# One group of value read-outs a pair, four buffers of each kind of exponentials, one dump tile, stack loads in odd steps

## The chip, the cores and the metric

The kernel runs on one core of a Trainium2 chip. The metric is the device time in microseconds (us) of one execution; each median below is over several executions. Beside the times there is one execution taken by the hardware profiler. The engines are TensorE (PE in the profile, with PEld for its weight loads), VectorE (DVE), ScalarE (ACT), GpSimd (POOL) and SyncE (SP). SP does no arithmetic here: it issues nearly all DMAs. SBUF is the on-chip memory of 128 partitions, PSUM the small memory that TensorE writes, in 8 banks of 128x512 fp32.

## What is computed

One transformer block on x of 2048 rows by 512 columns: modulated layer norm, attention with 32 heads of 16 columns in four segments of 512 rows, and a feed-forward part of width 1792. The part that matters here is the attention inside a segment:

```python
for s in range(N):                                   # 4 segments of L = 512 rows
    qs, ks, vs = q[:, :, s], k[:, :, s], v[:, :, s]
    logits = jnp.einsum("bhqd,bhkd->bhqk", qs, ks) * scale + mask
    p = _softmax(logits, axis=-1)
    a_dot = jnp.einsum("bhqk,bhkd->bhqd", p, vs)
    ...
    o = g * a_mem + (1.0 - g) * a_dot
```

## The kernel before

**Three parts.** Part A (up to about 190 us) makes q, k and v of all segments and writes q and k, split into three bf16 terms, to DRAM (`QD`, `KD`). Part B (about 180 to 480 us) is the attention above, with the output projection of finished segments and the preparation of the feed-forward part woven in. Part C is the feed-forward part. The change lies in part B alone.

**Steps and pairs.** Part B runs 64 steps P, four before them and two after; a step is two heads of one segment. Q = P // 2 numbers *pairs* of steps: four heads that share one stack of q rows and one of k rows (`qst`, `kst`, 96 rows of 2048 bf16, five buffers each, `NK = 5`). Eight pairs make a segment. What is issued in a step follows a list written out by hand, `PRM['order']` (lines 25 to 34): two lists for each segment, one for even and one for odd steps. Its tokens are

- `S0` to `S3` (`s_part`, line 623): the logits of step P + 4, with queries on the partitions, and their maximum over the keys. For each of the blocks 3, 2 and 1 of queries and each of the two heads TensorE makes a product of 512, 384 or 256 columns (line 610) and VectorE takes its masked maximum (`masked_max`, line 615): six maxima a step. Block 0 of all four heads shares a bank, a mask product and one plain maximum (`s_mask`, line 651), once a pair.
- `T0` to `T4` (`st_part`, line 702): the logits of step P again, keys on the partitions, with the maximum subtracted through three further rows of `qst` (lines 696 and 715); ScalarE writes their exponential into SBUF tiles `pts` of three kinds, GpSimd zeroes the causal triangle (line 699). Kind `pt0` holds key block 0, `pt1` blocks 1 and 3, `pt2` block 2.
- `c0` to `c9`: places for all else. Each item has a position, `ap(pos, f)`: step pos // 10, place pos % 10.

All `S` and `T` products rotate through six PSUM banks `att`. A bank is used again once its reader (VectorE for S, ScalarE for T) is done.

**The maximum and its dump tile.** `masked_max` is one VectorE operation that adds the mask, takes the minimum of the negated values into an accumulator and writes the elementwise result, which nobody reads, to a bf16 tile `dump`. On the engine it is two records: the operation itself (`CUSTOM_DVE_ANT_0`) and the read of the accumulator into `nm` (`DVE_READ_ACCUMULATOR2_ANT`), which raises VectorE's semaphore. The two tiles `dump0` and `dump1` take turns. In the instruction stream of the kernel before, a maximum waits for the count that the accumulator read of the maximum *two before it* raises, that is, for the last writer of its own dump tile; where it waits for TensorE too, that wait stands in an EVENT_SEMAPHORE instruction of its own ahead of it.

**The value read-out** (`pv_part`, line 731): for pair Q and key block j, four products, one for each head, of the exponentials with a 128x32 slice of `V`, each in its own 32 columns of the array and so beside one another; each fp32 product is two matmul instructions. Key block 0 has 512 columns, blocks 1, 2 and 3 have 384, 256 and 128. All accumulate in the bank `pvb`. `pv` lists for each segment the position (relative to 20 Q), key block and columns of the four blocks. With the table of before they form three separate runs on TensorE in the first segment (blocks 0 and 3; 2; 1) and two in the others (0 and 3, then 2 and 1; 0 and 2, then 1 and 3; 0, then 2, 1 and 3); the last pair forms one. `pv_out` (745, position `pvout`) copies the bank to `ts` on ScalarE and stores it to DRAM (`TD`); `pv_in` (753) loads two pairs back turned, `den` (773) makes the inverse denominator and stores it (`RD`), `rb_in` (782) loads it spread out.

**The row of maxima** (`m_rows`, 667, and `m_put`, 673): the maxima of pair Q, turned by TensorE, are copied by ScalarE to `ms` (48x128) and sent by a small DMA on ScalarE's own queue into rows 96 to 98 of `qst`, in step 2Q - 2. The first `T` of step 2Q needs it.

**The stack loads** (`load_stacks`, 190): `kst` and `qst` of pair Q, 384 KB each, from DRAM on SP, at position 20 Q + `stacks`. The first `S` that reads them stands in step 2Q - 4; the buffers' last readers are the `T` of step 2Q - 9. SP works its queue off in order and runs ahead of the steps as far as the waits allow.

Of the kernel before, what the change touches and what calls it, by code (L numbers as in the profile page):

```python
# [8 lines left out]
F32 = mybir.dt.float32  # L9
F32R = mybir.dt.float32r  # L10
BF16 = mybir.dt.bfloat16
# [23 lines left out]
 'turn': 2,  # L35
# [4 lines left out]
 'pvout': [41, 35, 34, 33],  # L40
 'mrows': [-21, -21, -25, -22],
 'mput': [-14, -15, -13, -13],
 'mrow0': -19,
 'mput0': -9,
 'stacks': -80,
 'den': [84, 84, 84, 84],
 'dnl': 11,
 'rbl': 7,
# [54 lines left out]
NEG = -1e30  # L103
# [3 lines left out]
def block_kernel(ctx: ExitStack, tc: tile.TileContext, x, wq, wk, wv, wo, betaq, betam,  # L107
                 w1, b1c, w2, b2, ccol, wmod, maskbd, mask8, out):
    nc = tc.nc
    v, act, pool, pe, sp = nc.vector, nc.scalar, nc.gpsimd, nc.tensor, nc.sync  # L110
# [7 lines left out]
    maskb = per.tile([128, 512], BF16, name="maskb")  # L118
# [101 lines left out]
    with ExitStack() as pa:  # L220
# [124 lines left out]
        for ds in ((0,), (1, 2, 3)):  # L345
# [4 lines left out]
            n = slice(ds[0], ds[-1] + 1)  # L350
# [180 lines left out]
        for s in range(NSEG):  # L531
            for tok in PRM["A"][s].split():
                n = int(tok[1]) if len(tok) > 1 and tok[1].isdigit() else 0
# [54 lines left out]
    with ExitStack() as pb:  # L588
        sb = pb.enter_context(tc.tile_pool(name="sb", bufs=2, reuse_waits="tile"))
# [15 lines left out]
        def bank():  # L605
            turn[0] += 1
            return att[turn[0] % 6]
# [1 line left out]
        def s_mm(ps, P, h, i):  # L609
            pe.matmul(ps, q_of(P, h, i), k_of(P, h, 128 * (i + 1)), start=True, stop=True)  # L610

        dump = [sb.tile([128, 512], BF16, name=f"dump{i}", bufs=1) for i in range(2)]
        n_dump = [0]

        def masked_max(dst, src, n):
            n_dump[0] += 1
            v.tensor_tensor_reduce(out=dump[n_dump[0] % 2][:, :n], in0=src, in1=maskb[:, 512 - n:], scale=-1.0, scalar=-4 * NEG,  # L617
                                   op0=ALU.add, op1=ALU.min, accum_out=dst)

        def s_max(dst, src):  # L620
# [59 lines left out]
        pts = {}  # L680
        late = []
# [12 lines left out]
        def st_mm(ps, P, h, j):  # L694
            q, k, e = qst[P // 2 % NK], kst[P // 2 % NK], 2 * (P % 2) + h
            pe.matmul(ps, k[:99, e, 128 * j:128 * j + 128], q[:99, e, 128 * j:512], start=True, stop=True)  # L696

        def causal(t, pattern):
            pool.affine_select(out=t, in_=t, pattern=pattern, compare_op=ALU.is_ge, fill=0.0,  # L699
                               base=0, channel_multiplier=-1)  # L700

        def st_part(P, part):
            ps = bank()
            if part < 4:
                u, h = part // 2, part % 2
                if (P, u) not in pts:
                    pts[P, u] = late[0].tile([128, 2, 512], F32, tag=f"pt{u}", bufs=3 + u, name=f"pt{P}_{u}")
                pt = pts[P, u]
                if u == 0:
                    st_mm(ps, P, h, 0)  # L710
                else:
                    st_mm(ps[:, :384], P, h, 1)
                    st_mm(ps[:, 384:], P, h, 3)
                    pts[P, 3] = pt[:, :, 384:]
                act.activation(pt[:, h, :], ps, AF.Exp, scale=0.25)  # L715
                if h == 1:
                    causal(pt[:, :, 0:128], [[0, 2], [1, 128]])
                    if u:
                        causal(pt[:, :, 384:], [[0, 2], [1, 128]])
            else:  # L720
                pt = late[0].tile([128, 2, 256], F32, tag="pt2", bufs=4, name=f"pt{P}_2")
                pts[P, 2] = pt
                two = ps.rearrange("k (h n) -> k h n", h=2)
                for h in range(2):
                    st_mm(two[:, h, :], P, h, 2)
                act.activation(pt, two, AF.Exp, scale=0.25)
                causal(pt[:, :, 0:128], [[0, 2], [1, 128]])
# [157 lines left out]
        for Q in range(32):  # L885
            z = Q // 8
            pv = PRM["pv"][z]
# [56 lines left out]
        for P in range(-LEAD, NP + 2):  # L944
            if P in PRM["w1at"]:
                stage_w1(2 * PRM["w1at"].index(P))
            for tok in PRM["order"][2 * min(P // 16, 3) + P % 2 if P >= 0 else 8 + P % 2].split():
                n = int(tok[1])
                if tok[0] == "S":
                    if P + LEAD < NP:  # L950
                        s_part(P + LEAD, n)
                elif tok[0] == "M":
                    s_mask()
                elif tok[0] == "T":
                    if 0 <= P < NP:
                        st_part(P, n)
                else:
                    for f, a in todo.pop((P, n), ()):
                        f(*a)
# [5 lines left out]
    with ExitStack() as pc:  # L965
# [127 lines left out]
        for n in range(AHEAD, NSEG * FB + AHEAD):  # L1093
            s, f = divmod(n, FB)
# [36 lines left out]
            if n < NSEG * FB:  # L1131
                if n > AHEAD:
                    ffn1(n)
                d = f - 9
# [58 lines left out]
```

## Time and profile before

| what | value |
|---|---|
| median of 3 runs (lowest, highest) | 809.91 us (808.03, 811.72) |
| time of the profiled execution | 815.29 us |
| its span, first to last instruction | 813.4 us |
| granted TensorE clock, mean of the span | 0.994 |
| ScalarE busy, GpSimd busy | 366.1 us (45%), 282.7 us (35%) |

The span is what the views divide into windows; the profiled execution took 1.9 us more than its span, and 5.4 us more than the median of the runs. Busy times are unions of an engine's records, so an engine that is 97% busy by them can still be the one that waits for nobody or one whose records merely touch. A window's row gives, for each engine, busy time and number of records, then the granted clock, the busy share of the DMA engines and what they moved.

### The profile page before, as it was taken

The page shows a single profiled execution, that of the slowest core. Times are in us where ns is not written, and L with a number is a line of the kernel's source. Part 1 is how long each engine was busy: PE and PEld are TensorE (multiplying, and loading weights), DVE is VectorE, ACT ScalarE, POOL GpSimd, SP SyncE. Part 2 cuts the span into 40 slices and gives each one's busy share as a digit, 9 for nine tenths or more (in the row PEclk, how much of TensorE's full clock was granted, in tenths as well). Part 3 has the DMA queues.
Part 4 walks back from the last instruction along what each step waited for, and adds up shares of the span by engine and source line. Part 5 has one row for each costly group of instructions (what it writes and reads, how often), then busy time and mean ns, then how long its engine had stood idle before and what let it go on. Part 6 is the DMA issues. An engine that isn't in the chain of part 4 may idle for free.

```text
span 813.4 us, 13418 instructions
## 1 busy us (share of the span) xinstructions
PE 790.9 (97%) x4637; PEld 549.1 (68%) x4637; DVE 505.9 (62%) x1353; ACT 366.1 (45%) x671; POOL 282.7 (35%) x496
## 2 busy tenths in 40 slices
PE   9999999999998999989999998999999999999998
PEld 4877767865443455435554556788888888888887
DVE  6685696458887887788779536884542353324223
ACT  4465645565777776667678661132112111211110
POOL 1347366541477565557878650000000000000000
PEclk9999999999999999999999999999999999999999
DMA  9597756496455577767656475733020121003001
GB/s 339 176 318 244 265 184 227 154 344 189 145 155 152 161 219 212 229 177 222 185 182 177 129 221 178 225 115 106 25 79 1 52 62 43 1 0 105 1 1 52
DMA packets 83564, 123.01 MB, mean 151 GB/s; under 512 B 14116, under 2 KB 46244, under 8 KB 82984
## 3 DMA queue, kind: packets, MB, share of 16 engines
q1 hardware_dynamic: 81000, 120.19, 47.2%
q10 hardware_dynamic: 2496, 1.97, 0.8%
q8 instruction: 36, 0.59, 0.3%
q14 instruction: 32, 0.26, 0.1%
HBM read 75.60 MB, written 46.15 MB: 150 GB/s over the span
## 4 chain that ended last, share of the span: by engine, by line
PE 47%; DVE 2%; DMA 2%; ACT 1%; issue 1%; SPq 0%; POOL 0%; DVEq 0%
PE acc L1075 18%; PE f1b L991 17%; PE pvb L740 3%; PE att L696 3%; PE mm L817 3%; PE att L610 2%; PE mm L162 1%; DMA xt<-X2D 1%; DMA w2r<-in_w 1%; DMA rm<-rdd 1%; PE mm L1075 1%; DVE dump L617 0%; DVE xb L835 0%; DVE cst L149 0%; ACT pt L715 0%
## 5 line engine op out<-in xcount | busy, mean ns | idle before, releaser
L617 DVE CUSTOM_DVE_ANT_0 dump<-att,maskb 128x512 bf16<-128x512 f32 (+2 forms) x384 | 192.2, 553 | 34.0 <-PE att L610 24.3
L715 ACT ACTIVATE pt<-att 128x512 f32<-128x512 f32 x256 | 144.2, 602 | 56.3 <-PE att L696 43.7
L994 ACT ACTIVATE gt<-f1b,b1t 128x512 f32<-128x512 f32 x56 | 38.5, 688 | 244.2 <-PE f1b L991 200.4
L699 POOL TENSOR_SCALAR_AFFINE_SELECT pt<-pt 128x256 f32<-128x256 f32 x256 | 99.7, 409 | 86.8 <-ACT pt L715 54.5
L140 DVE CAST gh<-gt 128x512 fp32r<-128x512 f32 x56 | 23.8, 426 | 161.3 <-ACT gt L994 161.3
L696 PE MATMUL att<-qst,kst 99*128 99x512 bf16 (+3 forms) x512 | 108.7, 305 | 8.8 <-DMA qst<-ms 5.4
L610 PE MATMUL att<-kst,qst 96*128 96x512 bf16 (+2 forms) x384 | 91.6, 331 | 0.7 <-DVE nm L617 0.2
L1075 PE MATMUL acc<-w2h,gh 128*128 128x512 f32 (+1 forms) x224 | 86.9, 388 | 0.0
L1075 PE MATMUL acc<-w2l,gh 128*128 128x512 f32 (+1 forms) x224 | 86.1, 384 | 0.8 <-DVE w2l L141 0.8
L696 PEld LDWEIGHTS <-kst 99*128 99x128 bf16 x512 | 44.8, 98 | 61.5 <-issue 26.8
L1075 PE MATMUL acc<-w2h,gl 128*128 128x512 f32 (+1 forms) x224 | 85.7, 383 | 0.0
L740 PE MATMUL pvb<-pt,V 128*32 128x512 f32 (+2 forms) x992 | 82.1, 442 | 0.0
L991 PE MATMUL f1b<-hodd,w1h 128*128 128x512 f32 x224 | 73.7, 390 | 0.0
L153 POOL TENSOR_SCALAR crs<-cmv 128x4 f32<-128x4 f32 x4 | 1.0, 248 | 172.6 <-DVE cmv L150 172.6
L740 PEld LDWEIGHTS pvb<-pt,V 128*32 128x32 f32 x992 | 25.0, 109 | 44.0 <-issue 39.8
L610 PEld LDWEIGHTS <-qst 96*128 96x128 bf16 x384 | 33.9, 99 | 23.9 <-issue 7.7
L1075 PEld LDWEIGHTS acc<-w2l,gh 128*128 128x128 f32 x224 | 42.1, 188 | 10.0 <-DVE w2l L141 1.6
L991 PEld LDWEIGHTS f1b<-hodd,w1h 128*128 128x128 f32 x224 | 42.1, 188 | 8.5
L1075 PEld LDWEIGHTS acc<-w2h,gl 128*128 128x128 f32 x224 | 42.1, 188 | 8.4
L1075 PEld LDWEIGHTS acc<-w2h,gh 128*128 128x128 f32 x224 | 42.1, 188 | 8.2
L991 PE MATMUL f1b<-C0hh,w1h 128*128 128x512 f32 x112 | 43.7, 390 | 0.8 <-DVE w1h L140 0.8
L991 PE MATMUL f1b<-C0hh,w1l 128*128 128x512 f32 x112 | 43.8, 391 | 0.3 <-DVE w1l L141 0.3
(213 smaller groups left out, 1546.0 us busy)
## 6 DMA issues: line engine op xcount, KB each, us to landing
kst<-KD SPq DMA_DIRECT2D x32, 384.0 KB
qst<-QD SPq DMA_DIRECT2D x32, 384.0 KB
TD<-ts SPq DMA_DIRECT2D x32, 256.0 KB
QD<-q SPq DMA_DIRECT2D x16, 384.0 KB
KD<-k SPq DMA_DIRECT2D x16, 384.0 KB
wm<-in_wmod SPq DMA_DIRECT2D x20, 256.0 KB
QD<-q SPq DMA_DIRECT2D x16, 256.0 KB
KD<-k SPq DMA_DIRECT2D x16, 256.0 KB
```

The lines of the kernel that those rows point to most:

```text
L140: v.tensor_copy(hi, src)
L162: pe.transpose(ps[:, 128 * b:128 * b + 128], xh[:, b, 128 * d:128 * d + 128], ident)
L610: pe.matmul(ps, q_of(P, h, i), k_of(P, h, 128 * (i + 1)), start=True, stop=True)
L617: v.tensor_tensor_reduce(out=dump[n_dump[0] % 2][:, :n], in0=src, in1=maskb[:, 512 - n:], scale=-1.0, scalar=-4 * NEG, op0=ALU.add, op1=AL ...
L696: pe.matmul(ps, k[:99, e, 128 * j:128 * j + 128], q[:99, e, 128 * j:512], start=True, stop=True)
L699: pool.affine_select(out=t, in_=t, pattern=pattern, compare_op=ALU.is_ge, fill=0.0, base=0, channel_multiplier=-1)
L715: act.activation(pt[:, h, :], ps, AF.Exp, scale=0.25)
L740: pe.matmul(ps[32 * c:32 * c + 32, lo:hi], V[4 * s + j][:, VW * hd:VW * hd + 32], pt[:, c % 2, lo - o:hi - o], start=start, stop=stop)
L817: pe.matmul(ps, a[:, 128 * b:128 * b + 128], w[:, g, :], start=(g == 0 and i == 0), stop=(g == 3 and i == 2))
L991: pe.matmul(ps, a[:, k, :], b[k], start=(i == 0), stop=(i == 11))
L994: act.activation(g, ps, AF.Gelu_apprx_tanh, bias=b1t[:, f:f + 1])
L1075: pe.matmul((mm if lo else acc[b])[:, lo:hi], a[:, c], w[:, lo:hi], start=(f == 0 and i == 0), stop=(last and i == 2))
```

## The change

The four key blocks of a pair are read out at one place, in the odd step 2Q + 3 (place 2 in the first segment, 3 in the others), in the order 0, 2, 1, 3, and the bank is copied out at the same place. Key block 0 is thereby read up to a step later, and `pt0` gets four buffers like the other kinds (one more, 4 KB a partition). `dump` is one tile (1 KB a partition less). The stack loads move from even to odd steps: position 20 Q - 70 in place of 20 Q - 80. `pv_in` keeps its distance of 11 places behind `pv_out`; `den` and all else keep their positions.

```diff
- 'pv': [[[29, 0, 0, 512], [29, 3, 384, 512], [32, 2, 256, 512], [41, 1, 128, 512]],
-        [[28, 0, 0, 512], [28, 3, 384, 512], [34, 2, 256, 512], [35, 1, 128, 512]],
-        [[29, 0, 0, 512], [29, 2, 256, 512], [33, 1, 128, 512], [34, 3, 384, 512]],
-        [[27, 0, 0, 512], [33, 2, 256, 512], [33, 1, 128, 512], [33, 3, 384, 512]]],
- 'pvout': [41, 35, 34, 33],
+ 'pv': [[[d, 0, 0, 512], [d, 2, 256, 512], [d, 1, 128, 512], [d, 3, 384, 512]] for d in (32, 33, 33, 33)],
+ 'pvout': [32, 33, 33, 33],
...
- 'stacks': -80,
+ 'stacks': -70,
...
-        dump = [sb.tile([128, 512], BF16, name=f"dump{i}", bufs=1) for i in range(2)]
+        dump = [sb.tile([128, 512], BF16, name="dump0", bufs=1)]
...
-            v.tensor_tensor_reduce(out=dump[n_dump[0] % 2][:, :n], in0=src, in1=maskb[:, 512 - n:], scale=-1.0, scalar=-4 * NEG,
+            v.tensor_tensor_reduce(out=dump[0][:, :n], in0=src, in1=maskb[:, 512 - n:], scale=-1.0, scalar=-4 * NEG,
...
-                    pts[P, u] = late[0].tile([128, 2, 512], F32, tag=f"pt{u}", bufs=3 + u, name=f"pt{P}_{u}")
+                    pts[P, u] = late[0].tile([128, 2, 512], F32, tag=f"pt{u}", bufs=4, name=f"pt{P}_{u}")
```

## The prediction

> **What bounds the kernel now.** I read the page first. Its row of busy times has the engines in the order PE, PEld, DVE, ACT, POOL:
>
> ```profile
> PE 790.9 (97%) x4637; PEld 549.1 (68%) x4637; DVE 505.9 (62%) x1353; ACT 366.1 (45%) x671; POOL 282.7 (35%) x496
> ```
>
> TensorE is busy 97% of the span, VectorE 62%. By these averages TensorE time is what counts and VectorE is free. But part B, where the change lies, has its own balance, so I cut it into stages by the work woven in: light pairs with attention alone, and heavy ones that also carry the output projection.
>
> ```profile
> core 0 of [0], span 813.4 us
> core 0: us, PE busy (x) PEld busy (x) DVE busy (x) ACT busy (x) POOL busy (x), PEclk, DMA share, GB/s
> 208.00:295.36 87.36, 83.23 (x728) 38.66 (x726) 74.22 (x284) 67.92 (x140) 55.65 (x125) 1.00 0.58 164
> 295.36:335.54 40.18, 40.08 (x309) 22.24 (x308) 30.23 (x111) 24.61 (x50) 21.64 (x47) 1.00 0.79 228
> 335.54:371.63 36.09, 32.51 (x268) 14.94 (x267) 30.60 (x113) 25.19 (x52) 20.30 (x46) 0.95 0.65 192
> 371.63:413.20 41.57, 40.88 (x318) 23.06 (x316) 29.82 (x109) 26.69 (x53) 34.51 (x56) 1.00 0.70 205
> 413.20:444.16 30.96, 30.82 (x278) 15.88 (x276) 29.66 (x107) 27.05 (x55) 23.94 (x49) 1.00 0.56 162
> 444.16:463.35 19.19, 19.19 (x152) 10.80 (x151) 14.65 (x49) 12.37 (x26) 12.72 (x25) 1.00 0.57 174
> 463.35:480.00 16.65, 15.86 (x130) 8.42 (x132) 2.68 (x5) 12.87 (x27) 12.34 (x23) 1.00 0.51 145
> ```
>
> I call these rows stages 1 to 7. The reader is to compare the PE and DVE columns with the length, the first number behind the window. Stages 1, 3 and 5 are light: VectorE is busy 74.22 of 87.36, 30.60 of 36.09 and 29.66 of 30.96 us. So there TensorE is the bound with VectorE close behind it; only in stages 2 and 4 has VectorE about 10 us to spare.
>
> **Part one, the groups: TensorE gains 9.2 us.** What does a run of read-outs cost beyond its columns? Start to start, a 512-column bf16 product takes 0.22 us before another ordinary product:
>
> ```profile
> 308.20 0.38 PE L654 MATMUL att<-maskb,identb 128*128 128x512 bf16 x1
> 308.42 0.27 PE L610 MATMUL att<-kst,qst 96*128 96x256 bf16 x1
> ```
>
> Before a read-out it takes 0.31 (310.01 to 310.32), so entering a run costs 0.09:
>
> ```profile
> 310.01 0.38 PE L696 MATMUL att<-qst,kst 99*128 99x512 bf16 x1
> 310.32 1.28 PE L740 MATMUL pvb<-pt,V 128*32 128x256 f32 x16
> 311.54 0.34 PE L696 MATMUL att<-qst,kst 99*128 99x384 bf16 x1
> ```
>
> That run is key blocks 2 and 1, 256 and 384 columns, and lasts 1.22. A run of the 384 columns alone lasts 0.78:
>
> ```profile
> 213.06 0.85 PE L740 MATMUL pvb<-pt,V 128*32 128x384 f32 x8
> 213.84 0.39 PE L696 MATMUL att<-qst,kst 99*128 99x512 bf16 x1
> ```
>
> So 256 columns joined to a run cost 0.44, 384 would cost 0.65, and the lone run carries 0.13 to 0.14 for leaving. Each run that is saved is worth 0.09 + 0.14 = 0.23 us. The table of positions gives 8 x 3 runs in the first segment, 8 x 2 in the second and one more where its last pair runs by the third's list, 8 x 2 in the third and 15 in the fourth, whose last pair is one run already: 72. Afterwards there are 32, so 40 are saved, 9.2 us. The joined run lasts 0.44 x 1280/256 + 0.14 = 2.3 us, in which VectorE and ScalarE get nothing new.
>
> **Part two, the stack loads: some us, if TensorE is still the bound.** TensorE's sequencer waits for the small DMA of the maxima:
>
> ```profile
> PEld L696 <- DMA qst<-ms: 13.4, 9, 3.5
> ```
>
> 13.4 us in nine waits is the most there is to win, but for the lower clock behind the longest (0.95 in stage 3). One of them: the 768 KB of stack loads go out just before the small DMA, and the product that needs it waits.
>
> ```profile
> 255.93 0.40 SPq L193 DMA_DIRECT2D kst<-KD  x1
> 256.38 1.51 SPq L193 DMA_DIRECT2D qst<-QD  x1
> ```
>
> ```profile
> 256.73 0.73 ACTq L678 DMA_DIRECT2D qst<-ms  x1
> ```
>
> ```profile
> 262.57 0.11 PEld L696 LDWEIGHTS <-kst 99*128 99x128 bf16 x2 [0.62 <-DMA qst<-ms]
> ```
>
> Moved ten places later, the load passes in SP's queue the items of the second half of the even step: alternately `pv_in`, which waits for the landing of `TD`, and the store of `den`, which waits for VectorE; in the later segments also `wo_x` and the store of `wo_out`. It then goes out behind the small DMA rather than ahead of it, so most of these waits should go. Being later costs nothing: the first stage holds 132.5 maxima (row below), six a step, 22 steps of 4.0 us. From load to first reader were four steps, 16 us; three are 12, and 768 KB at the 164 GB/s of that row take 4.7. The stage sums below already leave TensorE's idle time out, so this part enters as a cover, not as a term.
>
> **Part three, one dump tile: VectorE loses about 0.17 us a maximum.** Now every maximum waits for the one right before it. Free running looks so:
>
> ```profile
> 218.30 0.08 DVE L617 DVE_READ_ACCUMULATOR2_ANT nm<- 128x1 f32 x1
> 218.30 0.69 DVE L617 CUSTOM_DVE_ANT_0 dump<-att,maskb 128x512 bf16<-128x512 f32 x1
> 218.91 0.08 DVE L617 DVE_READ_ACCUMULATOR2_ANT nm<- 128x1 f32 x1
> 218.91 0.69 DVE L617 CUSTOM_DVE_ANT_0 dump<-att,maskb 128x512 bf16<-128x512 f32 x1
> ```
>
> The next maximum starts at 218.91 with the accumulator read, 0.08 before that read ends at 218.99. An operation that needs the result of its predecessor starts later. With the wait in the instruction itself:
>
> ```profile
> 248.59 0.35 DVE L775 RECIPROCAL dn<-dn 128x32 f32<-128x32 f32 x1 [0.42 <-DMA dn<-TD]
> 248.98 0.37 DVE L776 TENSOR_SCALAR dn<-dn,omg 128x32 f32<-128x32 f32 x1
> ```
>
> 0.04 after the end at 248.94; against -0.08 that is 0.12. Where the wait needs an EVENT_SEMAPHORE of its own:
>
> ```profile
> 474.63 0.69 DVE L789 TENSOR_TENSOR opk<-opk,rbB 128x512 f32<-128x512 f32 x1 [2.35 <-POOL pt L699]
> 475.43 0.70 DVE L791 TENSOR_TENSOR opk<-opk,amB 128x512 f32<-128x512 f32 x1
> ```
>
> 0.11 after the end at 475.32, so 0.19. Line 617 has 283 such instructions for its 384 maxima:
>
> ```profile
> L617 DVEq EVENT_SEMAPHORE  x283: 21/21/1767, 182.5 to 459.2; - x142
> ```
>
> Today they are done while the maximum before still runs, and cost nothing; with one tile they can't be. No row shows a maximum that waits for its neighbour, so the bounds are 0.12 and 0.19; I take the mix by this count, 0.74 x 0.19 + 0.26 x 0.12 = 0.17. What is queued behind a waiting maximum is all of VectorE's work; who waits for that is TensorE, through the six banks that S and T share, so it can't run more than a few products ahead.
>
> The Trainium skill weighs this otherwise: "VectorE: DVE Perf Modes", section "The DRAIN you can't avoid", has eight copies with a semaphore after each take as long as eight with one at the end, so the wait would cost nothing. The rows above disagree, 0.04 after the end against 0.08 before it; by the page the sum would be that of the first rival.
>
> **The sum.** Records of line 617 by stage, two a maximum:
>
> ```profile
> 208.00:295.36 87.36, 65.83 (x265) 1.00 0.58 164
> 295.36:335.54 40.18, 24.12 (x99) 1.00 0.79 228
> 335.54:371.63 36.09, 24.24 (x97) 0.95 0.65 192
> 371.63:413.20 41.57, 24.57 (x98) 1.00 0.70 205
> 413.20:444.16 30.96, 23.86 (x95) 1.00 0.56 162
> 444.16:463.35 19.19, 10.59 (x42) 1.00 0.57 174
> ```
>
> A stage afterwards lasts as long as its busier engine: VectorE's busy time plus 0.17 a maximum, or TensorE's less 0.23 a run saved.
>
> - Stage 1: VectorE 74.22 + 132.5 x 0.17 = 96.7; TensorE 83.23 less 19 runs = 78.9. 96.7 - 87.36 = **+9.4**.
> - Stage 2: VectorE 38.6, TensorE 40.08 - 0.9 = 39.2: **-1.0**.
> - Stage 3: VectorE 30.60 + 8.2 = 38.8, TensorE 31.5: **+2.8**, the long wait in it already counted away.
> - Stage 4: VectorE 38.1, TensorE 40.0; with its 0.7 idle kept **-0.9**.
> - Stage 5: VectorE 29.66 + 8.1 = 37.7, TensorE 29.9: **+6.8**.
> - Stages 6 and 7: TensorE less two runs each, **-0.5** and **-0.5**.
>
> Together +16.1. VectorE won't be full: in stage 5, where it nearly is, it idles 1.30 of 30.96, 4%. On the 173 us of stages 1, 3 and 5 that is up to 7 us, the more as the 2.3 us run starves it; I take half, 3.5. So +19.6: 834.9 against the profiled execution's own 815.3, and 829.5 against the median of 809.9, 5.4 below. The four steps before 208 us I count as nothing: their 36 maxima get dearer by 6 us, but the first small DMA waits there for transfers that would then be over.
>
> At nothing stand, too: the fourth `pt0` buffer (a product writes it only after the run that read it, on TensorE itself in that order), the copy `ts` that now holds ScalarE's queue for a whole run (ScalarE has 19.4 us idle in stage 1, 3.9 in stage 5; without that cover the run's 2.3 less the 1.2 of today's, 1 us a pair), and `pv_in`, which comes earlier in the first segment and so gives `den` more time.
>
> **Rivals.** *The wait is free* (the other side): maxima follow each other as now, VectorE keeps its busy times, TensorE takes 78.9, 31.5 and 29.9 in the light stages: -8.5 - 4.6 - 1.1 - 2.9 = -17, **793**; about 800 if the loads go out when they do now, since SP runs ahead, and the waits stay. In general the sum is -22.8 + 228.5 p for a price p a maximum: the change is slower from **p = 0.10 us** on. For it: today's semaphore instructions cost nothing. Against: the rows with a gap behind a dependent neighbour. *The low price*: all waits as cheap as 0.12 and no further idling, +4.6, **814**, or with a little help from the first steps no change. *Late stacks*: a load held behind `pv_in` comes after its first reader; each time as much as the worst of today's waits, 3.5 us; twice or more beyond the forecast, **840**. Against it stand 12 us for a transfer of 4.7.
>
> **How the numbers follow.** Forecast 0.72; free wait 0.13; low price 0.11; late stacks 0.04. The forecast's own range runs from 814 (0.12) to 839 (0.19 in stages 1, 3 and 5, +23.5, less 2.9, plus 7 and a little idling in stage 2: +29). To hold 8 in 10 it reaches down to the low price with some luck, 808, and up to 841. A measurement of this kernel tells about 0.5% from no change, so same is 806 to 814: faster 0.13, same 0.11, slower 0.76.
>
> **What would show it.** In the trace after: one L740 run of 32 instructions and 2.3 us a pair; each maximum starting 0.04 to 0.11 after the accumulator read in front of it; VectorE over 93% busy in stages 1, 3 and 5 and TensorE waiting there for DVE nm; the stack loads behind the small DMA and its waits gone. The prediction is wrong if maxima still start before the read in front ends, or if VectorE is late and TensorE does not wait for it.

## The result and the profile after

The median after is 874.85 us (four runs, 871.74 to 880.90), the ratio to the kernel before 1.0807, 95% interval 1.0772 to 1.0842. With a fourth run beside it the median before is 810.70, so the change costs 64 us. Slower was right; the forecast of 829.5 saw 20 of them, and the range ended at 841. In the run join_poolput below, some executions took over 1.5% more than the fastest one, and its time and ratio are those of the six others. The profiled execution took 871.74 us with a span of 870.0 and a mean granted clock of 0.976 (0.994 before). Its row of busy times:

```profile
PE 813.2 (93%) x4637; PEld 559.6 (64%) x4637; DVE 529.2 (61%) x1353; ACT 366.1 (42%) x671; POOL 281.0 (32%) x496
```

VectorE's busy time rose by 23.3 us, TensorE's by 22.3, and the span by 56.6: on each of the two, over half of the new time is idle time. Here are stages 1 to 6 of the kernel after, cut at the same distance behind the first `T` product of the same pairs as before (columns as in the prediction: window, length, busy time of PE, PEld, DVE, ACT and POOL, then the clock, the share of the DMA engines and GB/s):

```profile
209.50:318.80 109.30, 91.62 (x726) 42.71 (x724) 82.19 (x282) 67.93 (x139) 55.04 (x124) 0.95 0.49 140
318.80:364.30 45.50, 40.85 (x315) 23.55 (x314) 33.37 (x113) 24.20 (x50) 21.41 (x48) 1.00 0.59 172
364.30:407.60 43.30, 35.85 (x266) 16.23 (x265) 33.62 (x111) 25.30 (x51) 20.91 (x47) 0.88 0.57 174
407.60:456.60 49.00, 43.47 (x319) 24.01 (x318) 33.32 (x111) 26.63 (x53) 34.20 (x55) 0.97 0.51 153
456.60:495.50 38.90, 33.72 (x278) 16.89 (x276) 31.77 (x105) 27.41 (x55) 23.82 (x49) 0.96 0.56 155
495.50:518.00 22.50, 21.09 (x152) 11.68 (x151) 15.29 (x51) 12.25 (x26) 12.61 (x24) 0.92 0.44 138
```

| stage | length before | after | measured | predicted |
|---|---|---|---|---|
| 1 (light) | 87.36 | 109.30 | +21.9 | +9.4 |
| 2 (heavy) | 40.18 | 45.50 | +5.3 | -1.0 |
| 3 (light) | 36.09 | 43.30 | +7.2 | +2.8 |
| 4 (heavy) | 41.57 | 49.00 | +7.4 | -0.9 |
| 5 (light) | 30.96 | 38.90 | +7.9 | +6.8 |
| 6 | 19.19 | 22.50 | +3.3 | -0.5 |

Look at stage 2: TensorE is busy 40.85 of 45.50 us, VectorE 33.37. No engine is full, and yet the stage is 5 us longer. The forecast had no term for that.

The waits of the kernel after (engine, line waited for, total, times, longest; line numbers are three lower than before, so 614 is the maxima, 607 the `S` products, 693 the `T` products, 737 the read-outs):

```profile
ACT ts L129 <- PE pvb L737: 69.6, 30, 3.8
...
PE att L607 <- DVE nm L614: 22.5, 45, 1.4
PE att L693 <- DVE nm L614: 18.7, 36, 1.3
...
PEld L693 <- DMA qst<-ms: 1.7, 2, 1.3
PE att L693 <- DMA qst<-ms: 0.8, 1, 0.8
```

The waits for the small DMA are nearly gone (1.7 us where it was 13.4 before); TensorE waits for VectorE's maxima 81 times; ScalarE waits 69.6 us at the copy behind the read-outs. The maxima themselves, from the timeline of the kernel after (start, duration, record):

```profile
288.48 0.69 DVE L614 CUSTOM_DVE_ANT_0 dump<-att,maskb 128x512 bf16<-128x512 f32 x1
...
289.09 0.08 DVE L614 DVE_READ_ACCUMULATOR2_ANT nm<- 128x1 f32 x1
289.23 0.32 PE L607 MATMUL att<-kst,qst 96*128 96x384 bf16 x1 [0.52 <-DVE nm L614]
...
289.32 0.42 DVE L614 CUSTOM_DVE_ANT_0 dump<-att,maskb 128x256 bf16<-128x256 f32 x1
...
289.67 0.08 DVE L614 DVE_READ_ACCUMULATOR2_ANT nm<- 128x1 f32 x1
289.79 0.42 DVE L614 CUSTOM_DVE_ANT_0 dump<-att,maskb 128x256 bf16<-128x256 f32 x1
```

The accumulator read at 289.09 ends at 289.17; the next maximum starts at 289.32, 0.144 later by the exact records, where the wait has an EVENT_SEMAPHORE of its own; behind the read at 289.67 it starts 0.035 after the end, with the wait in the instruction. TensorE's product at 289.23 had waited 0.52 us for the first of these reads. Of the 384 maxima 325 come directly behind another one. 64 of these have the short gap; 261 have an EVENT_SEMAPHORE, and the gap is 0.144 in 207 of them, 0.173 in 23 and longer in 31, which waited for something else. Before, 272 of the 325 started ahead of the read's end, most by 0.08.

### The profile page after: what moved, and what is told of

Read it like the earlier page. It is cut to its first block, busy times and chain, and to the rows that moved or that the text cites. A ratio compares the mean times of both kernels' runs of the same rounds, so it can differ in the third digit from the quotient of the medians.

```text
span 870.0 us, 13429 instructions
## 1 busy us (share of the span) xinstructions
PE 813.2 (93%) x4637; PEld 559.6 (64%) x4637; DVE 529.2 (61%) x1353; ACT 366.1 (42%) x671; POOL 281.0 (32%) x496
## 4 chain that ended last, share of the span: by engine, by line
PE 76%; DVE 13%; issue 3%; DMA 3%; ACT 2%; POOL 1%; SPq 1%; DVEq 0%; POOLq 0%; ACTq 0%
PE acc L1072 16%; PE f1b L988 15%; PE pvb L737 9%; DVE dump L614 9%; PE att L693 6%; PE att L607 5%; PE q L328 5%; PE k L328 4%; PE mm L814 4%; PE v L479 3%; PE nu L451 1%; DMA xt<-X2D 1%; PE mm L159 1%; PE mp L428 1%; PE warm L294 1%
## 5 line engine op out<-in xcount | busy, mean ns | idle before, releaser
L614 DVE CUSTOM_DVE_ANT_0 dump<-att,maskb 128x512 bf16<-128x512 f32 (+2 forms) x384 | 213.7, 557 | 76.3 <-PE att L607 38.4
L607 PE MATMUL att<-kst,qst 96*128 96x512 bf16 (+2 forms) x384 | 100.9, 337 | 23.7 <-DVE nm L614 22.5
L693 PEld LDWEIGHTS <-kst 99*128 99x128 bf16 x512 | 47.0, 98 | 73.5 <-issue 50.1
L737 PE MATMUL pvb<-pt,V 128*32 128x512 f32 (+1 forms) x992 | 83.4, 481 | 0.0
L737 PEld LDWEIGHTS pvb<-pt,V 128*32 128x32 f32 x992 | 31.0, 118 | 57.4 <-issue 52.8
L129 ACT ACTIVATE ts<-pvb 128x512 f32<-128x512 f32 x31 | 18.5, 597 | 72.1 <-PE pvb L737 69.6
```

Source lines behind the costliest of these rows:

```text
L614: v.tensor_tensor_reduce(out=dump[0][:, :n], in0=src, in1=maskb[:, 512 - n:], scale=-1.0, scalar=-4 * NEG, op0=ALU.add, op1=ALU.min, accum ...
L737: pe.matmul(ps[32 * c:32 * c + 32, lo:hi], V[4 * s + j][:, VW * hd:VW * hd + 32], pt[:, c % 2, lo - o:hi - o], start=start, stop=stop)
```

## The experiments

Each run is compared with the kernel before on the same chip. The first theory was *the wait* (the maxima's new gap makes nearly all of the excess), its rival *the hole* (the 2.3 us run of read-outs starves VectorE, whatever the dump tile).

**One part alone.** First the dump tile alone, on the kernel before (lines as before):

```diff
-        dump = [sb.tile([128, 512], BF16, name=f"dump{i}", bufs=1) for i in range(2)]
+        dump = [sb.tile([128, 512], BF16, name="dump0", bufs=1)]
...
-            v.tensor_tensor_reduce(out=dump[n_dump[0] % 2][:, :n], in0=src, in1=maskb[:, 512 - n:], scale=-1.0, scalar=-4 * NEG,
+            v.tensor_tensor_reduce(out=dump[0][:, :n], in0=src, in1=maskb[:, 512 - n:], scale=-1.0, scalar=-4 * NEG,
```

> The kernel before with one dump tile in place of two, nothing else. Theory 'the wait' (a maximum that waits for its neighbour is the whole loss, 64 us): 865 to 880 us. Rival 'the hole' (the wait costs its 0.12 to 0.23 us a maximum in the light stages alone, about +17 to +30, and the rest of the 64 us comes from the 2.3 us run of read-outs that starves VectorE): 826 to 842 us. Either way maxima start 0.04 to 0.14 us after the accumulator read in front of them instead of 0.08 before its end.

839.64 against 810.94 us, ratio 1.0350 (1.0310 to 1.0390): +28.7 us. So the wait is less than half of the excess. Pairs 10 (light) and 14 (heavy), from the first `T` product to the next pair's, in the kernel before:

```profile
278.71:286.30 7.59, 7.59 (x66) 3.60 (x67) 7.03 (x27) 6.10 (x13) 5.68 (x11) 1.00 0.50 148
314.15:324.23 10.08, 10.08 (x80) 5.62 (x79) 8.01 (x28) 6.58 (x13) 6.69 (x13) 1.00 0.72 234
```

and in one_dump_only:

```profile
286.95:296.35 9.40, 8.01 (x68) 3.68 (x66) 7.94 (x28) 6.89 (x14) 5.95 (x12) 1.00 0.64 174
326.53:336.62 10.09, 10.09 (x79) 5.60 (x78) 8.38 (x28) 6.57 (x13) 6.68 (x13) 1.00 0.58 161
```

The heavy pair (second row) has TensorE busy throughout and keeps its length, as the forecast said. The light one is 1.8 us longer, and VectorE fills it: 7.94 us of work and 12 gaps of 0.12 make 9.4.

Then the change with two dump tiles (the memory for it comes from one buffer of `nm` and a pad):

```diff
-    ce.tile([128, 144], F32, name="cpad0")
...
-        nmt = [sb.tile([128, 8, 16], F32, name=f"nm{i}", bufs=1) for i in range(4)]
+        nmt = [sb.tile([128, 8, 16], F32, name=f"nm{i}", bufs=1) for i in range(3)]
...
-        dump = [sb.tile([128, 512], BF16, name="dump0", bufs=1)]
+        dump = [sb.tile([128, 512], BF16, name=f"dump{i}", bufs=1) for i in range(2)]
```

> The changed kernel with two dump tiles again; the 1 KB a partition comes from one buffer of maxima less (three for four) and a padding tile left out. Theory 'the wait': the loss is gone and the gain of the joined runs and of the later stack loads stays, 792 to 806 us. Rival 'the hole': the run alone still starves VectorE and ScalarE, 820 to 845 us.

841.41 against 810.94, 1.0385 (1.0336 to 1.0434): +30.5, and *the wait* has fallen as the whole cause. The joined run with its fourth buffer alone, on the kernel before with its own stack loads and two dump tiles (the memory comes from `nm` and the pad again; shown is what else differs from the kernel before):

```diff
+ 'pv': [[[d, 0, 0, 512], [d, 2, 256, 512], [d, 1, 128, 512], [d, 3, 384, 512]] for d in (32, 33, 33, 33)],
+ 'pvout': [32, 33, 33, 33],
...
-                    pts[P, u] = late[0].tile([128, 2, 512], F32, tag=f"pt{u}", bufs=3 + u, name=f"pt{P}_{u}")
+                    pts[P, u] = late[0].tile([128, 2, 512], F32, tag=f"pt{u}", bufs=4, name=f"pt{P}_{u}")
```

> The kernel before with the joined run of read-outs alone: two dump tiles, stack loads where they were, the fourth buffer paid for by one buffer of maxima less and a padding tile left out. Theory 'the hole' (a 2.3 us run leaves VectorE and ScalarE without new products, and they are late for the rest of the pair): about as slow as with the later loads too, 834 to 846 us. Rival 'it takes both' (the run costs nothing while the stack loads stand in the even steps): 800 to 812 us.

838.06 against 812.64, 1.0314 (1.0286 to 1.0341): +25.4. The missing buffer of `nm` can hardly be the cause here: maxima wait 2.4 us for GpSimd to have read `nm`, against 4.9 before. And the stack loads alone:

```diff
- 'stacks': -80,
+ 'stacks': -70,
```

> The kernel before with the stack loads ten places later, nothing else. Both theories: the small DMA of the maxima no longer stands behind the loads, TensorE's waits for it (13.4 us by the profile of before) fall to under 4 us, and the time falls by 4 to 10 us, to 800 to 806. A rival says SP runs ahead, the loads go out when they did, and nothing changes: 808 to 812.

810.83 against 810.94, 0.9982 (0.9955 to 1.0009): nothing that can be told. Its waits show why:

```profile
PEld L696 <- DMA qst<-ms: 5.9, 4, 2.6
...
PEld L610 <- DMA qst<-QD: 4.7, 3, 2.1
```

Of 13.4 us of waits for the small DMA 7.5 are gone, but products of `S` now wait 4.7 us for a stack that comes late, which is the mechanism of the rival *late stacks*, at 1.6 us a time instead of 3.5. So 28.7 and 25.4 to 30.5 us make 54 to 59 of the 64; the two parts nearly add.

Taking the dump tile away altogether, with the maximum written over its own source in PSUM, in the kernel after:

```diff
-            v.tensor_tensor_reduce(out=dump[0][:, :n], in0=src, in1=maskb[:, 512 - n:], scale=-1.0, scalar=-4 * NEG,
+            v.tensor_tensor_reduce(out=src, in0=src, in1=maskb[:, 512 - n:], scale=-1.0, scalar=-4 * NEG,
```

> The changed kernel without any dump tile: each maximum writes its elementwise result over the PSUM columns that it reads, so no maximum has to wait for its neighbour. Theory 'the wait': as with two dump tiles, 792 to 806 us, if the write to PSUM costs nothing; if that write makes a 512-column maximum longer than 0.69 us, slower by 384 times the difference in the stages where VectorE is the bound. Rival 'the hole': 820 to 845 us.

848.03, 1.0465 (1.0418 to 1.0513): better than one dump tile, worse than two. The trace shows the price: a maximum of 512 columns takes 0.723 us on average (0.685 in after_two_dumps) and the read of its accumulator 0.141 (0.082).

**What is dear in the joined run? Its length, or its place among the maxima?** All the following have two dump tiles; the diffs show the table `pv`, and `pvout` stands at the last place of each list. *halves* cuts the run in two of 1.22 us in the same odd step, *place* moves it whole:

```diff
- 'pv': [[[d, 0, 0, 512], [d, 2, 256, 512], [d, 1, 128, 512], [d, 3, 384, 512]] for d in (32, 33, 33, 33)],
+ 'pv': [[[32, 0, 0, 512], [32, 3, 384, 512], [35, 2, 256, 512], [35, 1, 128, 512]],
+        [[33, 0, 0, 512], [33, 3, 384, 512], [34, 2, 256, 512], [34, 1, 128, 512]],
+        [[33, 0, 0, 512], [33, 3, 384, 512], [35, 2, 256, 512], [35, 1, 128, 512]],
+        [[33, 0, 0, 512], [33, 3, 384, 512], [35, 2, 256, 512], [35, 1, 128, 512]]],
```

> The changed kernel with two dump tiles, its run cut into two of 1.22 us in the same odd step, with S and T products between them; everything else as in the run after_two_dumps (841 us). If the length of the one run makes the hole: 812 to 824 us, and VectorE's idle time of 1.4 us in a light pair falls to under 0.6. If reading out late, or all in the odd step, is what costs: 836 to 846 us.

843.35, 1.0378 (1.0353 to 1.0402): cutting it gained nothing. But the waits moved. In part B (208 to 480 us) VectorE's masked maxima wait 19.3 us for their products, where they waited 52.4 in after_two_dumps; the plain maximum of block 0 waits 15.8 (it was 1.6), and maxima wait 12.2 for GpSimd to have read `nm` (1.4). So the one buffer of `nm` less does count here, and what cutting is worth with four is not shown.

```diff
- 'pv': [[[d, 0, 0, 512], [d, 2, 256, 512], [d, 1, 128, 512], [d, 3, 384, 512]] for d in (32, 33, 33, 33)],
+ 'pv': [[[d, 0, 0, 512], [d, 2, 256, 512], [d, 1, 128, 512], [d, 3, 384, 512]] for d in (32, 34, 32, 35)],
```

> The changed kernel with two dump tiles, its one run moved to where more maxima are in work when it starts: behind S0 in segment 2, behind S1 and S0 in segment 3, behind S1 and S3 in segment 4; segment 1 as it was. If VectorE's work in hand at the start of the run decides how much of it VectorE idles: 822 to 834 us. If a run of 2.3 us costs the same anywhere: 838 to 846 us.

844.76, 1.0403 (1.0376 to 1.0429): nor did this move. *join_seg0* goes the other way: the kernel before, with its three runs a pair made two, and nothing read later than the odd step:

```diff
- 'pv': [[[29, 0, 0, 512], [29, 3, 384, 512], [32, 2, 256, 512], [41, 1, 128, 512]],
-        [[28, 0, 0, 512], [28, 3, 384, 512], [34, 2, 256, 512], [35, 1, 128, 512]],
-        [[29, 0, 0, 512], [29, 2, 256, 512], [33, 1, 128, 512], [34, 3, 384, 512]],
+ 'pv': [[[29, 0, 0, 512], [29, 3, 384, 512], [32, 2, 256, 512], [32, 1, 128, 512]],
+        [[28, 0, 0, 512], [28, 3, 384, 512], [34, 2, 256, 512], [34, 1, 128, 512]],
+        [[29, 0, 0, 512], [29, 2, 256, 512], [33, 1, 128, 512], [33, 3, 384, 512]],
```

> The kernel before with only the small runs joined that stand alone or next to each other: two runs a pair of at most 1.22 us everywhere, key block 0 read out where it was, two dump tiles, stack loads as before. 9 runs fewer at 0.23 us: 2 us faster by the price of a run, 806 to 811 us. If runs of 1.22 us already make holes: 812 or more.

808.36 against 812.64, 0.9948 (0.9929 to 0.9966): **faster than both kernels**, if by half a per cent. Joining paid here, where one run stayed early (in the first segment the copy `ts` comes nine places earlier, too). That led to a theory *each step for itself* and a rival *late*. *even_run* (on the kernel before, the whole run early) and *halves_apart* (on after_two_dumps, two runs late but one in each step; shown are the first and the last segment):

```diff
+ 'pv': [[[d, 0, 0, 512], [d, 2, 256, 512], [d, 1, 128, 512], [d, 3, 384, 512]] for d in (29, 28, 29, 27)],
```

> The kernel before with all four value blocks of a pair in one run, as after, but early, in the even step of the next pair (places 27 to 29) instead of the odd one (32, 33); two dump tiles, three and four pairs of exponentials, stack loads as before. Theory 'each step for itself' (a run of 2.3 us makes TensorE's step 4.7 us and leaves the other at 2.4, while VectorE needs 3.2 to 3.4 us in each, and six banks carry nothing over): 834 to 846 us, as in group_two_dumps with 838.06, and VectorE idle for 1 us or more in each even step. Rival 'late' (what costs is that the blocks of the even step are read five places later, in the odd step): 803 to 814 us, since nothing is later than before.

825.87 against 812.11, 1.0183 (1.0138 to 1.0228): between the two answers.

```diff
+ 'pv': [[[32, 0, 0, 512], [32, 3, 384, 512], [41, 2, 256, 512], [41, 1, 128, 512]],
...
+        [[33, 0, 0, 512], [33, 3, 384, 512], [39, 2, 256, 512], [39, 1, 128, 512]]],
```

> after_two_dumps with the run cut into two of 1.22 us, the first where the whole run stood (32, 33), the second in the even step after it (41, in the last segment 39), so later than in after_two_dumps. Theory 'each step for itself': the steps are even again, 3.6 us each, so 802 to 816 us, and light pairs of 7.5 to 7.8 us as before. Rival 'late': both halves are read as late as there or later, so 836 to 848 us, and light pairs of 8.4 us or more.

839.49, 1.0342 (1.0306 to 1.0378): even steps, no gain. *Each step for itself* has fallen. The next idea, *cover*, came from ScalarE's records. In the kernel after_two_dumps:

```profile
277.32 0.27 ACT L129 ACTIVATE ms<-mm 48x128 bf16<-48x128 f32 x1
277.62 0.73 ACTq L674 DMA_DIRECT2D qst<-ms  x1
...
278.37 0.32 PE L606 MATMUL att<-kst,qst 96*128 96x384 bf16 x1 [0.25 <-DVE nm L613]
278.39 0.60 ACT L711 ACTIVATE pt<-att 128x512 f32<-128x512 f32 x1 [0.81 <-PE att L606]
...
280.33 2.36 PE L736 MATMUL pvb<-pt,V 128*32 128x512 f32 x32
...
282.76 0.60 ACT L129 ACTIVATE ts<-pvb 128x512 f32<-128x512 f32 x1 [1.81 <-PE pvb L736]
...
283.27 0.69 DVE L613 CUSTOM_DVE_ANT_0 dump<-att,maskb 128x512 bf16<-128x512 f32 x1 [1.66 <-PE att L606]
```

The put of the maxima (copy and DMA issue) keeps ScalarE from exponentials for 1.08 us, 277.32 to 278.39, amid the products; two microseconds later, in the run, ScalarE stands idle for 1.81 and VectorE for 1.66. In join_seg0 the put lies beside the run, and VectorE works right through it:

```profile
263.97 0.28 ACT L132 ACTIVATE ms<-mm 48x128 bf16<-48x128 f32 x1
...
264.20 0.69 DVE L617 CUSTOM_DVE_ANT_0 dump<-att,maskb 128x512 bf16<-128x512 f32 x1
264.28 0.73 ACTq L678 DMA_DIRECT2D qst<-ms  x1
264.29 1.28 PE L740 MATMUL pvb<-pt,V 128*32 128x512 f32 x16
...
264.81 0.42 DVE L617 CUSTOM_DVE_ANT_0 dump<-att,maskb 128x256 bf16<-128x256 f32 x1
265.06 0.60 ACT L715 ACTIVATE pt<-att 128x512 f32<-128x512 f32 x1 [0.81 <-PE att L696]
265.16 0.42 DVE L617 CUSTOM_DVE_ANT_0 dump<-att,maskb 128x256 bf16<-128x256 f32 x1
```

Three runs move only that cover. *early_before* is join_seg0 with the first run at place 24, ahead of the put:

```diff
+ 'pv': [[[24, 0, 0, 512], [24, 3, 384, 512], [32, 2, 256, 512], [32, 1, 128, 512]],
+        [[24, 0, 0, 512], [24, 3, 384, 512], [34, 2, 256, 512], [34, 1, 128, 512]],
+        [[24, 0, 0, 512], [24, 3, 384, 512], [33, 2, 256, 512], [33, 1, 128, 512]],
+        [[24, 0, 0, 512], [24, 3, 384, 512], [33, 2, 256, 512], [33, 1, 128, 512]]],
```

> join_seg0 (808.36 us, 0.9948 of before) with the first run of each pair moved ahead of the put of the maxima in the same even step (place 24 instead of 27 to 29; the last segment's three joined blocks divided two and two as in the others); the second run stays at 32 to 34. Nothing is read later than there, and each step still has one run. Theory 'cover': 820 to 840 us, with TensorE waiting for banks behind each put. Rival 'late', and theory 'each step for itself' too: 803 to 814 us.

827.61 against 811.43, 1.0182 (1.0130 to 1.0234): +19 us over join_seg0 for some five places, as *cover* said; nothing is read later. Another reading would be that the read-outs now come too early for their exponentials; TensorE waited 1.8 us for that, so it is not much of the 19. *late_even* is halves_apart with its second run behind the put:

```diff
- 'pv': [[[32, 0, 0, 512], [32, 3, 384, 512], [41, 2, 256, 512], [41, 1, 128, 512]],
+ 'pv': [[[32, 0, 0, 512], [32, 3, 384, 512], [48, 2, 256, 512], [48, 1, 128, 512]],
```

> halves_apart with only the second run moved, in three of four segments from place 41 to 48 of the even step, so that it stands right behind the put of the maxima, and later still. Theory 'cover' (a run must stand where ScalarE spends 1.08 us on the copy and the DMA issue of the maxima and makes no exponentials): 803 to 818 us and light pairs of 7.5 to 7.8 us. Rival 'late' (what is read out later costs): 838 to 852 us.

885.61, 1.0908 (1.0851 to 1.0964), above both ranges, by a new wait: exponentials for which no buffer is free, since the read-outs now come so late.

```profile
ACT pt L714 <- PE pvb L739: 42.6, 24, 2.2
```

*after_mput* moves the put in after_two_dumps:

```diff
- 'mput': [-14, -15, -13, -13],
+ 'mput': [-9, -9, -9, -9],
```

> after_two_dumps (841.41 us) with the put of the maxima moved from places 5 to 7 of the even step to place 1 of the odd step, right ahead of the joined run, which stays late and in one piece. Theory 'cover': 816 to 830 us, near even_run with 825.87, where the joined run stands behind the put, and ScalarE's idle time in the run shrinks by about 1 us a pair. Rivals 'late' and 'each step for itself': 836 to 848 us.

862.18, 1.0600 (1.0526 to 1.0675), above both ranges too: put later, the small DMA comes too late.

```profile
PEld L692 <- DMA qst<-ms: 26.2, 12, 5.4
...
PE att L692 <- DMA qst<-ms: 19.7, 10, 5.0
```

So neither of these two says anything of *cover*. The next two shorten the put instead of moving it, in after_two_dumps and in join_seg0:

```diff
-            act.dma_start(qst[Q % NK][96:99], ms)
+            pool.dma_start(qst[Q % NK][96:99], ms)
```

> after_two_dumps (841.41 us) with the small DMA of the maxima issued by GpSimd instead of ScalarE, so that ScalarE is away from the exponentials for about 0.35 us a pair (the copy) instead of 1.08. Theory 'cover': TensorE's waits behind the put shrink, 818 to 834 us, unless the DMA comes late (waits for qst from ms far above 4 us would say so). Rival (the place matters for another reason than the put): 837 to 846 us.

844.46 against 811.04, 1.0410 (1.0379 to 1.0442): no gain, as the rival of *cover* said. ScalarE is back at the exponentials 0.25 us after the copy starts, and TensorE waits all the same, for VectorE:

```profile
278.21 0.27 ACT L129 ACTIVATE ms<-mm 48x128 bf16<-48x128 f32 x1
278.46 0.60 ACT L711 ACTIVATE pt<-att 128x512 f32<-128x512 f32 x1
...
279.27 0.32 PE L606 MATMUL att<-kst,qst 96*128 96x384 bf16 x1 [0.25 <-DVE nm L613]
```

The test is not clean, though: VectorE's small product `dn` takes 0.944 us on average in part B here, 0.551 in after_two_dumps.

> join_seg0 (0.9948 of before) with the small DMA of the maxima issued by GpSimd instead of ScalarE. Theory 'cover': the put already lies beside the first run of each pair, so shortening it gains little: 802 to 811 us, a small fraction of what after_poolput gains. Rival (shortening the put is worth the same everywhere): below before by the same 10 to 20 us as after_poolput, so 790 to 800 us.

816.71, 1.0061 (1.0018 to 1.0105): above both ranges, not faster; its waits for the small DMA rose to 14.7 and 11.2 us (7.2 and 5.0 in join_seg0).

*early_close* moves the two runs of join_seg0 close together:

```diff
+ 'pv': [[[29, 0, 0, 512], [29, 3, 384, 512], [31, 2, 256, 512], [31, 1, 128, 512]],
+        [[28, 0, 0, 512], [28, 3, 384, 512], [30, 2, 256, 512], [30, 1, 128, 512]],
+        [[29, 0, 0, 512], [29, 3, 384, 512], [31, 2, 256, 512], [31, 1, 128, 512]],
+        [[27, 0, 0, 512], [27, 3, 384, 512], [30, 2, 256, 512], [30, 1, 128, 512]]],
```

> join_seg0 with the second run of each pair moved up close to the first (places 30 or 31 instead of 32 to 34), so two runs of 1.22 us with one to three products between, the first behind the put of the maxima; the last segment's three joined blocks divided two and two. Theory 'length' (what is left of the joined run's cost is that it is 2.3 us in one piece): 805 to 814 us. Rival 'nearness' (the banks are not full again before the second run): 818 to 830 us, like even_run.

821.54, 1.0141 (1.0104 to 1.0179): inside the range of *nearness*. Last, VectorE's work is cut, by leaving half of the scores of the widest blocks out of their maxima:

```diff
-            v.tensor_tensor_reduce(out=dump[n_dump[0] % 2][:, :n], in0=src, in1=maskb[:, 512 - n:], scale=-1.0, scalar=-4 * NEG,
+            lo = n - 256 if n == 512 else 0
+            v.tensor_tensor_reduce(out=dump[n_dump[0] % 2][:, :n - lo], in0=src[:, lo:], in1=maskb[:, 512 - n + lo:], scale=-1.0, scalar=-4 * NEG,
```

> after_two_dumps (841.41 us) with the widest maxima, four a pair, taken over the last 256 of their 512 columns (0.34 us instead of 0.61); half of those scores is left out of the maxima. Theory 'VectorE makes the pair' (its work plus the time that it stands idle in the run): 1.07 us less a pair, down to TensorE's own 7.3 or so, so 812 to 824 us. Rival (banks, ScalarE or the run itself hold TensorE up): 834 to 846 us.

830.56 against 811.55, 1.0227 (1.0171 to 1.0283): a gain of 11 us, between the two ranges, where 34 us were taken from VectorE (128 maxima at 0.685 less 0.419). In part B TensorE's waits for VectorE's maxima fall from 16.2 us in after_two_dumps to 5.8, and those for ScalarE's exponentials rise from 0.9 to 5.0. At the same products as above VectorE is in time, and now ScalarE's put holds TensorE:

```profile
277.58 0.27 ACT L129 ACTIVATE ms<-mm 48x128 bf16<-48x128 f32 x1
...
278.66 0.60 ACT L712 ACTIVATE pt<-att 128x512 f32<-128x512 f32 x1 [0.81 <-PE att L606]
...
279.31 0.38 PE L693 MATMUL att<-qst,kst 99*128 99x256 bf16 x2 [0.33 <-ACT pt L712]
```

> join_seg0 (0.9948 of before) with the same shorter maxima. By both theories TensorE is the bound of the split kernel's pairs already: 798 to 809 us, at most a third of what after_short_max gains. If it gains as much as after_short_max, VectorE is no more the bound of the joined run than of the split one.

807.77, 0.9955 (0.9932 to 0.9979), the same as join_seg0: there VectorE doesn't set the pace.

**Read together.** Four kernels form a square: first run behind the put or not, one run or two. They differ in little else (buffers of `pt0` and `nm`, how the last segment is divided, and the place of `ts`, which follows the last run).

| | two runs | one run |
|---|---|---|
| first run behind the put | join_seg0 0.9948 | even_run 1.0183 |
| elsewhere | early_before 1.0182 | group_two_dumps 1.0314 |

Pairs 10 (light) and 14 (heavy) of these, from the views by window. join_seg0:

```profile
277.57:285.08 7.51, 7.51 (x67) 3.54 (x66) 7.11 (x28) 6.38 (x15) 6.10 (x13) 1.00 0.57 180
312.58:322.65 10.07, 10.07 (x79) 5.61 (x79) 8.02 (x28) 6.58 (x13) 6.73 (x13) 1.00 0.65 179
```

even_run:

```profile
276.62:284.75 8.13, 7.54 (x67) 3.85 (x67) 7.02 (x28) 6.00 (x14) 5.33 (x12) 1.00 0.58 169
315.87:325.70 9.83, 9.83 (x80) 5.80 (x79) 8.01 (x28) 6.58 (x13) 7.09 (x13) 1.00 0.55 158
```

early_before:

```profile
279.55:288.06 8.51, 7.81 (x68) 3.60 (x66) 7.01 (x27) 6.38 (x14) 5.70 (x12) 1.00 0.49 158
318.81:329.92 11.11, 10.44 (x80) 5.61 (x79) 7.92 (x28) 6.61 (x13) 6.65 (x13) 1.00 0.55 171
```

group_two_dumps:

```profile
281.52:290.05 8.53, 7.72 (x68) 3.82 (x67) 6.96 (x28) 6.35 (x14) 5.95 (x12) 1.00 0.66 159
320.63:331.62 10.99, 10.45 (x80) 5.86 (x79) 7.91 (x28) 6.37 (x13) 7.06 (x13) 1.00 0.59 172
```

In the heavy pair only the place counts: behind the put even the joined run leaves TensorE busy throughout, and at 9.83 it saves the quarter microsecond that the forecast gave it; elsewhere the pair costs 1 us more. In the light pair each costs (8.51 for the place, 8.13 for joining, 7.51 with neither), but not one on top of the other: 8.53 for both. So these two pairs don't show where group_two_dumps loses its further 10 us; 6 of them lie behind the last read-out of the profiles (340.1 us from there to the end, 334.2 in early_before), which no run explains.

## Why the prediction was right or wrong

**The maximum's price: right, by two errors that cancel.** It was taken as 0.17 us for every maximum, the mix by today's count of semaphore instructions, between bounds of 0.12 and 0.19. Measured, the next maximum starts 0.035, 0.144 or 0.173 us after the read's end against 0.082 ahead of it, so it loses 0.117, 0.226 or 0.255, and most are of the dear kinds: 0.205 on average over the 294 that wait for nothing else. But only 325 of 384 maxima come directly behind another one, and 0.205 x 325 / 384 is 0.17 again. That the two errors meet is luck. By the forecast's own sum (9.4 + 2.8 + 6.8 in stages 1, 3 and 5) the tile alone costs 19.0. Cut at the same exponentials as in the profile of before, these stages are 10.2, 2.2 and 5.4 us longer in one_dump_only, 17.8 together; stages 2 and 4, which were to lose nothing by it, are 0.7 and 3.1 longer. With smaller differences elsewhere this makes the 22.9 by which the two spans differ (836.3 less 813.4); the medians differ by 28.7, since the profiled execution of before lay 4 us above the 810.94 and that of one_dump_only 1 below its own median. So the step "a stage lasts as long as its busier engine" holds for this part to some 3 us a stage.

The Trainium skill ("VectorE: DVE Perf Modes", section "The DRAIN you can't avoid") has a semaphore after each of a chain of copies cost nothing. For these maxima it doesn't hold: the same operation moves from 0.08 us before its neighbour's end to as much as 0.17 behind it.

**The joined run: the step that failed.** The forecast let it save 9.2 us of TensorE and put what it starves at half of 4% idle, 3.5 us. Alone it cost 25.4. Stage 1 shows the error: VectorE's 82.19 us and its short gaps, 12.9 us in pieces of at most 0.2, make 95, close to the 96.7 of the sum; but the stage lasts 109.3. Of VectorE's 13 us of idle time before (87.36 less 74.22) the sum had spent all, but for the 3.5 us in the three light stages together, and 14 are there afterwards. 13 of them touch a run of read-outs or the half microsecond behind it, and so did 12.6 of the 13 before. Idle time in a stage was treated as a reserve; but it lay where TensorE gave VectorE nothing new, and six banks did not carry work there. The copy `ts` was put at nothing, with ScalarE's idle time as cover, and at 1 us a pair without it. The average pair lost 0.8 (25.4 us by 31 pairs), and ScalarE's waits for the read-outs are 69.6 us (8.9 before), so the cover was not there; how much of the loss is the copy's is not shown, since no run moves it away from the run's end.

What sets that loss is only half settled. Shown: the place of the first run is worth 19 us to split runs and 11 to 12 to a joined one (the square's columns, 827.61 less 808.36 and 838.06 less 825.87, the latter 11 by the ratios); joining in the early place costs 17 to 19; taking work from VectorE gives 11 us in the joined kernel and none in the split one; two runs close together cost nearly as much as one (early_close gains 4). Seen in two traces, but not tried together: behind the put TensorE waits for whichever of VectorE and ScalarE is later, and when one is relieved the other is in its place (after_poolput, after_short_max). A kernel with both relieved wasn't run, and why two runs at places 33 and 41 cost as much as one stays open. So that the joined run costs, and how much, is shown; by what chain of waits is in part argued.

**The heavy stages: wrong.** TensorE-bound on average, they were to gain 1 us each and lost 5.3 and 7.4. Most of that is the joined run's: in group_two_dumps these stages are 3.0 and 6.8 us longer than before, in one_dump_only 0.7 and 3.1. VectorE works 7.91 of the 10.99 us of their pair 14 there, and TensorE is not full either. The run itself saved what it was to save, 0.25 us in pair 14 of even_run; what was missing is the time that the other engines lose by it.

**The stack loads: right.** They were entered as cover only, and alone they change nothing. In the kernel after, the waits for the small DMA are gone; on the kernel before they were traded for waits of the rival *late stacks*, which has the mechanism and not the size.

**The other rivals.** *The wait is free* and *the low price* needed gaps that cost nothing or 0.12 everywhere; the rows and one_dump_only exclude both. (The 840 of *late stacks* stands for three waits of 3.5 us; two make 836.5.) What was announced as marks came in part: one run a pair, the gaps, TensorE waiting for `nm`. VectorE over 93% in the light stages did not come: with its gaps it fills 95 of 109.3 us in stage 1, 87%; the other 14 are the hole.

## What to carry to other kernels

Where engines hand work through a few banks, don't add an engine's work over a stage: ask, for each stretch in which the producer does something else, how much work the banks hold for each consumer, and what else the consumer has to do just then. Try a producer's long foreign work beside a consumer's foreign work, and not all of it in one place: here the read-outs stood best right behind ScalarE's put, in two runs. A scratch tile that nobody reads still orders its writers; a second one was worth 28.7 us here. And look where an engine is idle before counting its idle time as a reserve.

## What was not expected of the hardware

A wait that needs an instruction of its own cost 0.11 us more than one carried in the instruction, 0.144 against 0.035, though the semaphore instruction's record is 0.021 us long. And short stalls of TensorE were followed by half its clock. The trace of the kernel after has ten stretches of 3.4 or 6.8 us at half clock inside part B; one of them and the 3.4 us ahead of it (window, length, busy times; the clock is the third number from the end):

```profile
266.12:269.53 3.41, 2.57 (x14) 1.13 (x13) 2.80 (x11) 2.54 (x7) 2.61 (x6) 1.00 0.10 28
269.53:272.94 3.41, 3.27 (x18) 0.90 (x21) 2.62 (x10) 1.02 (x3) 1.15 (x4) 0.50 0.83 207
```

In the 3.4 us ahead TensorE stood idle for 0.84 us; ahead of the ten it was 0.8 to 1.8. Idle time alone does not decide it below 1.4 us. Cut on the same grid of 3.41 us from 205 us on, all five windows at full clock with over 1.4 us of idle time were followed by half clock, but only four of the 22 with 0.8 to 1.3. This one, idle for 1.24 us, was followed by full clock:

```profile
300.25:303.66 3.41, 2.17 (x19) 0.98 (x20) 3.05 (x13) 2.62 (x6) 1.57 (x6) 1.00 0.06 11
```

The kernel before has two such stretches there. Ahead of one TensorE had been idle for 1.5 us, ahead of the other for nearly the whole window:

```profile
349.96:353.37 3.41, 0.15 (x1) 0.11 (x2) 2.40 (x9) 0.43 (x1) 3.25 (x7) 1.00 0.11 32
```

The Trainium skill ("TensorE: Matmul & The Clock Gate", section "What's actually happening") has the clock fall after an idle window of about 3.4 us. That fits this last row, and none of the ten. The page's section "A second HAM failure mode: psum-queue depth-cycling" has short idle times between groups of products bring the clock down, too. The ten agree with it.

What the stretches cost can be estimated: they last 40.9 us together, 10.2 before, and the difference at half speed is 15 us of TensorE's 22.3 us of new busy time. They add to the excess but don't make it: halves_apart has a mean clock of 1.000 and still takes 839.49 us.
